# Early projections in 64-row tiles over two banks each, and an own bank for the last half block

## The chip, the cores and the metric

One Trainium2 chip, one core of it. The metric is the device time of one execution in microseconds. Matrix products run on TensorE (PE in the profile), with weight loads listed apart (PEld). VectorE is DVE, ScalarE is ACT, GpSimd is POOL, and SyncE (SP) issues the transfers. "Banks" are the eight accumulation banks (PSUM) of 128 partitions by 512 floats, which PE writes and DVE and ACT read.

## The reference

A mixer layer on x of shape 1 x 2048 x 512, in float32: layer norm, sliding-window attention with 32 heads of width 16 and a window of 256, and a gated channel MLP beside it.

```python
    x = A_x
    xn = _layernorm(x, axis=-1)
    s = _A_ref(xn, A_wqkv, A_wo)            # qkv = xn @ wqkv; softmax over the window; o @ wo
    g = _silu(_B_ref(xn, B_w1, B_b1, B_w2, B_b2))   # layer norm again, gelu(y @ w1 + b1) @ w2 + b2
    return x + s * g
```

## The kernel before

**Arithmetic.** Products with float32 accuracy are made of three passes over operands split into a high and a low part (`PASSES`). A projection job is therefore 12 matmuls of 512 columns (four slices of 128 rows times three passes) or 24 of 256.

**Slots.** The attention runs in slots t = 0 to 127, one block of 128 keys of one group of four heads each. `prob_block` makes scores (`stb`), which ACT turns into exponentials (`pt`) and POOL masks. `max_block(m)`, twelve slots ahead (`LEAD = 12`, m = t + 12), makes scores for the row maxima: four matmuls into `xy`, four into `zo`, then on DVE a masked copy (`COPY_PREDICATED`) and a `TENSOR_REDUCE`. `xy` is one tile, so the next block's matmuls wait for that reduction. Slots -16 to -1 have no exponentials; there the maxima of the first group are found while the first projections are made.

**Fill work.** The projections are cut into pieces and hung into half slots (t, 0) and (t, 1) in the table `fills`: `job_qk(n, c)` projects queries and keys of head group n for the 512 tokens of chunk c, `job_v(hf, i)` projects values for 256 tokens, and `job_x(c)` transposes the normalised x of chunk c, which the projections of that chunk need. A job's `finish` copies the result out of its bank; `later(k, ...)` puts a step k half slots on. For `job_qk(0, c)` the high part is cast by ACT and the low part subtracted by DVE straight from the bank, so the bank is free only behind both.

**Order.** Every engine but SP runs its instructions in the order in which the code was written; nothing is rescheduled. A step that waits holds back all that stands behind it on its engine.

**Banks.** `xy`, `zo` and `fb[0]`, `fb[1]` hold two, two and one each; before slot 0 the pool `ps_st` has two more, which become `stb` at slot 0.

**Rows of the array.** The score matmuls (`xy`, most of `zo`, `stb`) use tiles of 64 rows, two of which run side by side on the two halves of the array. From slot 3 on `tandem` runs two projection jobs in the same way: in a first phase the lower rows of one job and the upper rows of the other, in a second phase the reverse, into `fb[0]` and `fb[1]`. Ahead of slot 3 the projections use all 128 rows.

**The end.** `end_chunk` multiplies the attention's result by wo, 12 matmuls for a block of 128 tokens, and DVE gates it. The last block is cut in two halves of 256 columns, both in one tile `ps`, so that the first can be gated and sent while the second is made.

## Time and profile before

| what | us |
|---|---|
| median of three runs | 737.28 (737.04 to 737.39) |
| the profiled execution, its own time | 736.97 |
| its span in the trace | 735.2 |
| PE busy in the span | 722.8 |
| slots -8 to -1 (start of the first fill of -8 to the first `stb`) | 34.1 to 61.8 |
| slots 0 to 2 | 61.8 to 71.5 |

All times of the trace count from the start of the span. A line of the timeline gives start, length, engine, line, operation, output and inputs, shape and count, and in brackets the idle time before it and what ended it. All instructions pass through one helper (L43), so groups are told apart by tile names: `fb`, `pv` and `tr` are banks of projections and transposes, `pjr` and `sh` the low and high parts of a query and key projection, `xnT` the transposed x, `vt` the values, `wqb` and `wva` weights.

### The profile page before, as it was taken

The page shows a single profiled execution, that of the slowest core. Times are in us where ns is not written, and L with a number is a line of the kernel's source. Part 1 is how long each engine was busy: PE and PEld are TensorE (multiplying, and loading weights), DVE is VectorE, ACT ScalarE, POOL GpSimd, SP SyncE. Part 2 cuts the span into 40 slices and gives each one's busy share as a digit, 9 for nine tenths or more (in the row PEclk, how much of TensorE's full clock was granted, in tenths as well). Part 3 has the DMA queues.
Part 4 walks back from the last instruction along what each step waited for, and adds up shares of the span by engine and source line. Part 5 has one row for each costly group of instructions (what it writes and reads, how often), then busy time and mean ns, then how long its engine had stood idle before and what let it go on. Part 6 is the DMA issues. An engine that isn't in the chain of part 4 may idle for free.

```text
span 735.2 us, 18562 instructions
## 1 busy us (share of the span) xinstructions
PE 722.8 (98%) x7344; PEld 583.7 (79%) x7344; DVE 498.4 (68%) x736; ACT 425.3 (58%) x713; POOL 315.8 (43%) x669
## 2 busy tenths in 40 slices
PE   8999999999999999999999999999999999999997
PEld 7886777777778888777776788888888888888886
DVE  7886777877766676777872657446787855667823
ACT  7757777868777676788877736232343734541001
POOL 7413757867677665777877540203302000001102
PEclk9999999999999999999999999999999999999999
DMA  8333356877676733677624367447223312263701
GB/s 286 88 68 76 84 144 167 224 213 222 200 202 177 209 113 107 158 178 205 177 82 143 129 230 181 162 130 243 86 58 115 115 59 86 67 191 112 247 14 58
DMA packets 61526, 106.74 MB, mean 145 GB/s; under 512 B 12096, under 2 KB 12352, under 8 KB 61440
## 3 DMA queue, kind: packets, MB, share of 16 engines
q1 hardware_dynamic: 61440, 105.56, 49.1%
q8 instruction: 58, 0.95, 0.5%
q14 instruction: 28, 0.23, 0.1%
HBM read 54.53 MB, written 33.82 MB: 120 GB/s over the span
## 4 chain that ended last, share of the span: by engine, by line
PE 93%; ACT 3%; DVE 2%; issue 1%; DMA 1%; SPq 0%; DVEq 0%; ACTq 0%
PE fb L43 20%; PE acc L43 20%; PE zo L43 14%; PE stb L43 9%; PE p L43 9%; PE s L43 6%; PE h L43 6%; PE xy L43 6%; PE pv L43 3%; ACT pt L43 2%; DMA x<-in_x_dram 1%; DVE xy L43 0%; PE tr L43 0%; DVE xnT L43 0%; ACT x L43 0%
## 5 line engine op out<-in xcount | busy, mean ns | idle before, releaser
L43 POOL TENSOR_SCALAR_AFFINE_SELECT pt<-pt 128x256 f32<-128x256 f32 x480 | 192.9, 426 | 121.2 <-ACT pt L43 116.0
L43 ACT ACTIVATE pt<-stb 128x768 f32<-128x768 f32 (+1 forms) x244 | 188.7, 773 | 45.2 <-PE stb L43 38.3
L43 DVE TENSOR_REDUCE mt<-xy 128x4 f32<-128x1024 f32 (+1 forms) x128 | 152.6, 1192 | 4.4
L43 DVE COPY_PREDICATED xy<-upper,zo 128x512 f32<-128x512 int32 x112 | 77.8, 695 | 74.2 <-PE xy L43 66.8
L43 POOL TENSOR_TENSOR xo<-xo,gated 128x512 f32<-128x512 f32 x15 | 19.9, 1330 | 221.5 <-DVE gated L43 220.5
L43 PE MATMUL fb<-xnT,wqb 64*128 64x512 f32 (+1 forms) x684 | 106.6, 397 | 0.1
L43 PE MATMUL zo<-pt,vt 128*17 128x128 f32 x2880 | 103.6, 275 | 0.0
L43 PE MATMUL stb<-qk 64*128 64x384 f32 (+1 forms) x488 | 95.0, 384 | 5.1 <-ACT pt L43 4.0
L43 PE MATMUL acc<-w,gh 128*128 128x512 f32 x320 | 98.5, 389 | 0.0
L43 PEld LDWEIGHTS stb<-qk 64*128 64x128 f32 x488 | 45.7, 183 | 50.0 <-ACT pt L43 40.9
L43 PEld LDWEIGHTS zo<-pt,vt 128*17 128x17 f32 x2880 | 67.5, 97 | 15.2 <-issue 4.9
L43 PEld LDWEIGHTS fb<-xnT,wqb 64*128 64x128 f32 (+1 forms) x684 | 64.6, 185 | 8.7 <-issue 0.6
L43 PEld LDWEIGHTS acc<-w,gh 128*128 128x128 f32 x320 | 60.1, 188 | 12.5
L43 PE MATMUL acc<-w,gl 128*128 128x512 f32 x160 | 62.4, 390 | 0.2 <-DVE gl L43 0.2
L43 PE MATMUL xy<-qk 64*128 64x256 f32 (+2 forms) x536 | 58.5, 291 | 0.2 <-DVE mt L43 0.2
L43 PEld LDWEIGHTS xy<-qk 64*128 64x128 f32 x536 | 46.6, 185 | 6.8 <-issue 3.1
L43 PE MATMUL p<-xnT 128*128 128x512 f32 x189 | 51.8, 389 | 0.0
L43 ACT COPY oraw<-zo 128x128 f32<-128x128 f32 x108 | 28.7, 266 | 38.3 <-PE zo L43 29.3
L43 ACT ACTIVATE gated<-acc 128x512 f32<-128x512 f32 x16 | 8.7, 596 | 62.4 <-DVE acc L43 62.4
L43 PE MATMUL s<-wos,ohl 128*128 128x512 f32 (+1 forms) x204 | 44.3, 376 | 0.0
L43 PEld LDWEIGHTS s<-wos,ohl 128*128 128x128 f32 x204 | 36.8, 188 | 7.1
L43 PEld LDWEIGHTS p<-xnT 128*128 128x128 f32 x189 | 35.5, 188 | 7.4
(178 smaller groups left out, 1156.5 us busy)
## 6 DMA issues: line engine op xcount, KB each, us to landing
qk<-sh SPq DMA_DIRECT2D x128, 128.0 KB
qk<-pjr SPq DMA_DIRECT2D x64, 128.0 KB
oT_d<-oraw SPq DMA_DIRECT2D x32, 256.0 KB
w_d<-in_w_dram SPq DMA_DIRECT2D x14, 512.0 KB
xt_d<-xnT SPq DMA_DIRECT2D x12, 512.0 KB
x<-in_x_dram SPq DMA_DIRECT2D x16, 256.0 KB
w<-w_d SPq DMA_DIRECT2D x16, 256.0 KB
or<-oT_d SPq DMA_DIRECT2D x16, 256.0 KB
```

The lines of the kernel that those rows point to most:

```text
L43: r = issue(*args, **kwargs)
```

## The change

From slot -8 on, every projection up to slot 2 is run by the new `by_halves`. A job's 512 columns (or two blocks of 256) lie in two banks. In the first phase a unit is a matmul of the upper 64 rows into the second bank and one of the lower 64 rows into the first; in the second phase the rows change banks. A job is then 24 units of two matmuls of 64 rows by 256 columns. Between the phases stands a hand-over: POOL sets one column of `sv` to zero once the first phase's last two matmuls are through, and the second phase's first two wait for that.

```diff
+    def by_halves(job, banks, first, second):
+        half, finish, box = job
+        box[:] = banks
+        seen = []
+        for phase, where in enumerate((first, second)):
+            for i in range(12):
...
+                    two = (half(box[1 - phase], 1 - phase, i, slice(64, P), **flags),
+                           half(box[phase], phase, i, slice(0, 64), **flags))
+                    if phase == 0 and i == 11:
+                        seen.append(nc.gpsimd.memset(sv[:, 31:32], 0.0))
+                        for r in two:
+                            tc.add_manual_dep(seen[0].ins, r.ins.name, ORDER, reason="the rows are through")
+                    if phase == 1 and i == 0:
+                        for r in two:
+                            tc.add_manual_dep(r.ins, seen[0].ins.name, ORDER, reason="the banks change rows")
+                fills.setdefault(where[len(where) * i // 12], []).append((unit, ()))
+        fills[second[-1]].append((finish, ()))
```

The jobs' places are written out in pairs, whose phases alternate:

```diff
-    groups = [(4 * c - 16, 4, group(c)) for c in range(NCH)]
-    for t0, n, jobs in groups:
-        fills.update(spread(jobs, [(t0 + i // 2, i % 2) for i in range(2 * n - (t0 == -4))]))
-    fills[-8, 0] += fills[-8, 1][:4]
-    del fills[-8, 1][:4]
+    for c in range(2):
+        fills.update(spread(group(c), [(4 * c - 16 + i // 2, i % 2) for i in range(8)]))
...
+    others = [free_bank, free_bank]
+    for job, banks, first, second in (
+            (job_qk(0, 2), fb, [(-8, 0)], [(-7, 0)]), (job_v(0, 4), others, [(-8, 1)], [(-7, 1)]),
+            (job_v(0, 5), fb, [(-5, 0)], [(-4, 0)]), (job_qk(0, 3), others, [(-5, 1)], [(-4, 1)]),
+            (job_v(0, 6), fb, [(-3, 0)], [(-2, 0)]), (job_qk(1, 0), others, [(-3, 1)], [(-2, 1)]),
+            (job_v(0, 7), fb, [(-1, 0)], [(-1, 1)]), (job_qk(1, 1), fb, [(0, 1), (1, 0)], [(2, 0), (2, 1)])):
+        by_halves(job, banks, first, second)
+    fills.update(spread([job_x(3)], [(-6, 0), (-6, 1)]))
```

The transposes of the last chunk, `job_x(3)`, use `fb[0]` and `fb[1]` for their first two quarters (the second and third before) and `ps_st` for the other two. A job's `finish` copies from two banks with two instructions. For `job_qk(1, 0)` and `(1, 1)` the copies were one instruction each. Before, `job_qk(1, 0)` and `(1, 1)` were spread over slots -2 to 2: 10 of their 24 matmuls stood ahead of slot 0. Now `(1, 0)` ends in slot -2 and `(1, 1)` begins in slot 0.

The last block's second half goes to a tile of another pool:

```diff
-            ps = ps_st.tile([P, 512], F32, tag="b", name=f"s_{c}_{i}")
+            halves = []
             for cols in parts:
                 k = 0
+                ps = (ps_yt if halves else ps_st).tile([P, 512], F32, tag="b", name=f"s_{c}_{i}_{len(halves)}")
+                halves.append(ps)
...
-                    nc.vector.tensor_mul(gated[:, i, h], ps[:, h], gated[:, i, h])
+                    nc.vector.tensor_mul(gated[:, i, h], halves[q][:, h], gated[:, i, h])
```

Three places of the order of instructions, before and with the change. Words in brackets name the engines or transfers for which an instruction waits.

POOL, from the end of slot -9: the layer norm of the last chunk (`x_93` is the tile with its tokens), and what follows it. Before:

```order
L43 TENSOR_SCALAR ve_3_565<-sums 128x1 [waits Activation_49]
L43 TENSOR_TENSOR rss<-ve_3_565,mhalf 128x1 [waits Pool_49]
L43 TENSOR_SCALAR x_93<-x_93,nm_230,rss 128x512 [waits DMAHW1_49]
L43 TENSOR_SCALAR x_93<-x_93,nm_230,rss 128x512 [waits DMAHW2_49,Pool_49]
L43 AFFINE_SELECT pt_0_1_868<-pt_0_1_868 128x2x128 [waits Activation_49]
```

With the change:

```order
L43 TENSOR_SCALAR ve_3_565<-sums 128x1 [waits Activation_49]
L43 TENSOR_TENSOR rss<-ve_3_565,mhalf 128x1 [waits Pool_49]
L43 TENSOR_SCALAR x_93<-x_93,nm_230,rss 128x512 [waits DMAHW1_49]
L43 TENSOR_SCALAR x_93<-x_93,nm_230,rss 128x512 [waits DMAHW2_49,Pool_49]
L43 MEMSET sv 128x1 [waits PE_49]
L43 MEMSET sv 128x1 [waits PE_49,Pool_49] x6
L43 AFFINE_SELECT pt_0_1_1100<-pt_0_1_1100 128x2x128 [waits Activation_49]
```

The seven hand-overs ahead of slot 0 stand behind the layer norm on POOL; the eighth follows among the selections.

PE, slots -6 and -5: the transposes of the last chunk with the maxima of m = 6 between, and the first matmuls behind them. Before (`pv_4`, `pv_5` are the values' tiles, `tr` are tiles of `ps_st`, `fb_111` and `fb_112` the two `fb` banks):

```order
L43 MATMUL pv_4_607<-wva,xnT 128x256 x12
L43 MATMUL tr_0_646<-ident,x_93 128x128 [waits Activation_49,Pool_49]
L43 MATMUL tr_0_646<-ident,x_93 128x128 [waits Pool_49] x3
L43 MATMUL fb_111<-ident,x_93 128x128 x4
L43 MATMUL xy<-qk_94 128x256 [waits DVE_49]
L43 MATMUL xy<-qk_94 128x256 x3
L43 MATMUL zo<-qk_94 128x128 x4
L43 MATMUL fb_112<-ident,x_93 128x128 x4
L43 MATMUL tr_3_675<-ident,x_93 128x128 [waits Activation_49]
L43 MATMUL tr_3_675<-ident,x_93 128x128 x3
L43 MATMUL pv_5_683<-wva,xnT 128x256 [waits DVE_49]
```

With the change:

```order
L43 MATMUL fb_111<-ident,x_93 128x128 [waits DVE_49]
L43 MATMUL fb_111<-ident,x_93 128x128 x3
L43 MATMUL fb_112<-ident,x_93 128x128 [waits DVE_49]
L43 MATMUL fb_112<-ident,x_93 128x128 x3
L43 MATMUL xy<-qk_94 128x256 x4
L43 MATMUL zo<-qk_94 128x128 x4
L43 MATMUL tr_2_734<-ident,x_93 128x128 [waits Activation_49]
L43 MATMUL tr_2_734<-ident,x_93 128x128 x3
L43 MATMUL tr_3_741<-ident,x_93 128x128 [waits Activation_49]
L43 MATMUL tr_3_741<-ident,x_93 128x128 x3
L43 MATMUL fb_112<-wva,xnT 128x256 [waits DVE_49]
```

The first two quarters now go to the banks that the query and key job has just left, and the values' job behind the transposes begins in the banks of these two quarters.

DVE, from the reduction of m = 4 to that of m = 6. Before:

```order
L43 TENSOR_REDUCE mt_4_586<-xy 128x4 [waits DVE_49]
L43 TENSOR_TENSOR pjr_2_600<-fb_112,sh_2_599 128x512 [waits Activation_49]
L43 COPY_PREDICATED xy<-upper,zo 128x4x128 [waits DVE_49,PE_49]
L43 TENSOR_REDUCE mt_4_586<-xy 128x4 [waits DVE_49]
L43 TENSOR_TENSOR xnT<-tr_0_646,xnT 128x512 [waits Activation_49]
L43 COPY_PREDICATED xy<-upper,zo 128x4x128 [waits DVE_49,PE_49]
L43 TENSOR_REDUCE mt_4_586<-xy 128x4 [waits DVE_49]
L43 TENSOR_TENSOR xnT<-fb_111,xnT 128x512 [waits Activation_49]
```

With the change:

```order
L43 TENSOR_REDUCE mt_4_601<-xy 128x4 [waits DVE_49]
L43 COPY_PREDICATED xy<-upper,zo 128x4x128 [waits DVE_49,PE_49]
L43 TENSOR_REDUCE mt_4_601<-xy 128x4 [waits DVE_49]
L43 TENSOR_TENSOR pjr_2_664<-fb_111,sh_2_663 128x256 [waits Activation_49]
L43 TENSOR_TENSOR pjr_2_664<-fb_112,sh_2_663 128x256 [waits Activation_49]
L43 TENSOR_TENSOR xnT<-fb_111,xnT 128x512 [waits Activation_49]
L43 COPY_PREDICATED xy<-upper,zo 128x4x128 [waits DVE_49,PE_49]
L43 TENSOR_REDUCE mt_4_601<-xy 128x4 [waits DVE_49]
L43 TENSOR_TENSOR xnT<-fb_112,xnT 128x512 [waits Activation_49]
```

The subtraction that frees the query and key job's banks stands one reduction later, in two instructions; the one that frees the second transposed quarter's bank still stands behind the reduction of m = 6.

More of the change, by code (lines that the diff above doesn't have):

```diff
@@ L233, in mm @@
             if i == 0:
-                box.append([fb[0], fb[1], zo[:, 0], None][kt] if c == 1 and kt < 3 else fill_bank() if c > 1 and kt in (1, 2) else
+                box.append([fb[0], fb[1], zo[:, 0], None][kt] if c == 1 and kt < 3 or c == 3 and kt < 2 else
+                           fill_bank() if c == 2 and kt in (1, 2) else
                            ps_st.tile([P, 512], F32, tag="b", name=f"tr_{c}_{kt}"))
@@ L297, in mm @@
             if i == 0:
-                box.append(fill_bank() if n or c else xy[:, 0])
+                box.append(fill_bank() if c else xy[:, 0])
             kt, a, b = ops[i]
@@ L301, in mm, with half @@
                              start=(i == 0), stop=(i == len(ops) - 1))
+        def half(bank, j, i, r, **flags):
+            kt, a, b = ops[i]
+            return nc.tensor.matmul(bank[:, 0:256], wqs[n][r, a, kt],
+                                    big[r, b, kt, 512 * c + 256 * j: 512 * c + 256 * (j + 1)], **flags)
         def send(src, qk, tt):
@@ L309, in finish @@
             lo = raw.bitcast(F32R)
-            src = raw if n else box[0]
             if n:
-                nc.scalar.copy(raw, box[0])
+                for j, bank in enumerate(box):
+                    nc.scalar.copy(raw[:, 256 * j: 256 * (j + 1)], bank[:, 0:256])
+                box[:] = [raw]
+            wide = 512 // len(box)
+            parts = [(bank[:, 0:wide], slice(wide * j, wide * (j + 1))) for j, bank in enumerate(box)]
             def high():
-                nc.scalar.copy(hi, src)
+                for src, at_ in parts:
+                    nc.scalar.copy(hi[:, at_], src)
                 behind(now[0], send_high)
@@ L322, in low @@
             def low():
-                (nc.gpsimd if n else nc.vector).tensor_tensor(lo, src, hi.bitcast(F32), op=ALU.subtract)
+                for src, at_ in parts:
+                    (nc.gpsimd if n else nc.vector).tensor_tensor(lo[:, at_], src, hi[:, at_].bitcast(F32),
+                                                                  op=ALU.subtract)
                 behind(now[0], send_low)
@@ L330, in finish, with unit @@
             later(1 if n else 0, high)
-            later(3 if n else 1, low)
+            later(3 if n else int(c < 3), low)
+        if n or c > 1:
+            return half, finish, box
         return [(216, mm, i) for i in range(len(ops))], finish
+    def by_halves(job, banks, first, second):
[4 more added lines that the diff above has]
+            for i in range(12):
+                flags = dict(start=(phase == 0 and i == 0), stop=(phase == 1 and i == 11), skip_group_check=True)
+                def unit(i=i, phase=phase, flags=flags):
+                    if phase == 0 and i == 0:
+                        box[:] = [bank() if callable(bank) else bank for bank in box]
+                    two = (half(box[1 - phase], 1 - phase, i, slice(64, P), **flags),
[9 more added lines that the diff above has]
+        fills[second[-1]].append((finish, ()))
     def job_v(hf, i):
@@ L344, in mm, with half @@
                              start=(k % 12 == 0), stop=(k % 12 == 11))
+        def half(bank, j, k, r, **flags):
+            kt, (a, b) = k // 3, PASSES[k % 3]
+            kb = 2 * i + j
+            return nc.tensor.matmul(bank[:, 0:256], big[r, a, kt, P * kb: P * (kb + 1)], wva[r, b, kt], **flags)
         def finish():
-            nc.scalar.copy(vt[:, 2 * i: 2 * i + 2, :, 0:DH], box[0].rearrange("p b (h d) -> p b h d", d=DH))
+            if i < 4:
+                nc.scalar.copy(vt[:, 2 * i: 2 * i + 2, :, 0:DH], box[0].rearrange("p b (h d) -> p b h d", d=DH))
+                return
+            for j, bank in enumerate(box):
+                nc.scalar.copy(vt[:, 2 * i + j, :, 0:DH], bank[:, 0:256].rearrange("p (h d) -> p h d", d=DH))
+        if i > 3:
+            return half, finish, box
         return [(109, mm, k) for k in range(24)], finish
@@ L741, in group, with free_bank @@
             return [job_qk(0, 0), job_v(0, 0), (ops[:12] + x_ops, lambda: None), (ops[12:], finish)]
-        return [job_qk(0, c), job_v(0, 2 * c), *([job_x(c + 1)] if c + 1 < NCH else []), job_v(0, 2 * c + 1)]
-    groups = [(4 * c - 16, 4, group(c)) for c in range(NCH)]
-    for t0, n, jobs in groups:
-        fills.update(spread(jobs, [(t0 + i // 2, i % 2) for i in range(2 * n - (t0 == -4))]))
-    fills[-8, 0] += fills[-8, 1][:4]
-    del fills[-8, 1][:4]
+        return [job_qk(0, c), job_v(0, 2 * c), job_x(c + 1), job_v(0, 2 * c + 1)]
+    for c in range(2):
+        fills.update(spread(group(c), [(4 * c - 16 + i // 2, i % 2) for i in range(8)]))
+    def free_bank():
+        return ps_st.tile([P, 512], F32, tag="b", name=f"pair_{now[0]}")
+    others = [free_bank, free_bank]
[6 more added lines that the diff above has]
+    fills.update(spread([job_x(3)], [(-6, 0), (-6, 1)]))
     fills[-10, 0][:0] = fills[-11, 1][-5:]
     del fills[-11, 1][-5:]
-    for place, todo in spread([job_qk(1, 0), job_qk(1, 1)], [(-2, 0), (-1, 1), (-1, 1), (-1, 1), (0, 0), (0, 1)] +
-                              [(t, k) for t in (1, 2) for k in range(2)]).items():
-        fills.setdefault(place, []).extend(todo)
-    fills[0, 1].insert(0, fills[0, 0].pop())
     soon = {}
```

## The prediction

> **What bounds the kernel now.** First the page: the busy shares and the chain that ended last.

> ```profile
> span 735.2 us, 18562 instructions
> PE 722.8 (98%) x7344; PEld 583.7 (79%) x7344; DVE 498.4 (68%) x736; ACT 425.3 (58%) x713; POOL 315.8 (43%) x669
> PE 93%; ACT 3%; DVE 2%; issue 1%; DMA 1%; SPq 0%; DVEq 0%; ACTq 0%
> ```

> PE is the bound nearly everywhere, so what PE loses in a slot is found again at the end. But the change sits in two stages, and there I read the busy times by windows: the columns are PE, PEld, DVE, ACT and POOL.

> ```profile
> 34.10:61.80 27.70, 27.70 (x212) 23.79 (x210) 22.24 (x31) 16.42 (x24) 5.58 (x12) 1.00 0.27 60
> 61.80:71.50 9.70, 9.68 (x79) 5.70 (x78) 6.59 (x10) 6.66 (x11) 4.99 (x11) 1.00 0.36 86
> ```

> In slots -8 to -1 PE is busy without a gap for 27.70 us, but DVE is close behind with 22.24. Whatever makes PE faster there can bring 5.5 us at most, and any order in which PE and DVE wait for each other by turns brings less. The timeline of PE shows the places (start, length, what):

> ```profile
> 33.86 0.33 PE L43 MATMUL zo<-qk 64*128 64x128 f32 x4
> 34.12 2.56 PE L43 MATMUL fb<-xnT,wqb 128*128 128x512 f32 x10
> 36.61 0.50 PE L43 MATMUL xy<-qk 64*128 64x256 f32 x4
> 36.95 0.34 PE L43 MATMUL zo<-qk 64*128 64x128 f32 x4
> 37.22 0.72 PE L43 MATMUL fb<-xnT,wqb 128*128 128x512 f32 x2
> ...
> 41.48 0.60 PE L43 MATMUL tr<-ident,x 128*128 128x128 f32 x4
> ...
> 42.44 0.51 PE L43 MATMUL xy<-qk 64*128 64x256 f32 x4
> 42.78 0.34 PE L43 MATMUL zo<-qk 64*128 64x128 f32 x4
> 43.05 0.66 PE L43 MATMUL fb<-ident,x 128*128 128x128 f32 x4
> 43.55 0.60 PE L43 MATMUL tr<-ident,x 128*128 128x128 f32 x4
> 43.90 1.67 PE L43 MATMUL pv<-wva,xnT 128*128 128x256 f32 x12
> ...
> 61.81 0.44 PE L43 MATMUL stb<-qk 64*128 64x384 f32 x2
> ...
> 71.53 0.44 PE L43 MATMUL stb<-qk 64*128 64x384 f32 x2
> ```

> **What the change saves on PE.** The new unit, two matmuls of 64 x 256 side by side, already runs later in the kernel, next to score matmuls of 64 rows:

> ```profile
> 71.81 0.40 PE L43 MATMUL xy<-qk 64*128 64x256 f32 x4
> 72.04 1.08 PE L43 MATMUL fb<-xnT,wqb 64*128 64x512 f32 x8
> ...
> 97.43 0.37 PE L43 MATMUL zo<-qk 64*128 64x128 f32 x4
> 97.60 1.17 PE L43 MATMUL fb<-xnT,wqb 64*128 64x512 f32 x8
> ...
> 233.96 1.12 PE L43 MATMUL fb<-wva,xnT 64*128 64x256 f32 x16
> 234.92 0.34 PE L43 MATMUL stb<-qk 64*128 64x384 f32 x2
> ```

> Eight units from 233.96 to 234.92: 0.12 us each, so a half job of 12 is 1.44 and a job 2.88. A values' job of 24 matmuls of 128 rows has about the same pace (12 in 1.67 with the last one's tail). Ten matmuls of a query and key job took 2.49 (34.12 to 36.61), so a job about 3.0. The gain is in the changes: ahead of 64-row work `xy` costs 0.23 from start to start (71.81 to 72.04), behind 128-row work 0.34 (36.61 to 36.95); `zo` costs 0.17 (97.43 to 97.60) against 0.27 (36.95 to 37.22). A block of maxima `xy` + `zo` is thus 0.40 instead of 0.61. Eight such blocks in slots -8 to -1, all but the one between the transposes: 7 x 0.21 = 1.5 us, and the two fills of each of slots 0 to 2 change rows too, about as often (6 x 0.2 = 1.2). About 2.7 us is what there is to gain on PE.

> **What it makes PE wait for.** I put the new order on the old clock, from 33.86 on. The first half of `job_qk(0, 2)` runs from 34.03 to 35.47. The next `xy` needs the reduction of m = 3:

> ```profile
> 34.97 1.23 DVE L43 TENSOR_REDUCE mt<-xy 128x4 f32<-128x1024 f32 x1
> ```

> It ends at 36.20, so `xy` starts at 36.25, 0.8 lost; before it started at 36.61 anyway. With `zo` to 36.65; the first half of `job_v(0, 4)` to 38.09. Now the second half of the query and key job waits for the hand-over on POOL, and POOL is not free:

> ```profile
> 38.42 0.19 POOL L43 TENSOR_SCALAR ve<-sums 128x1 f32<-128x1 f32 x1
> 38.70 0.55 POOL L43 TENSOR_TENSOR rss<-ve,mhalf 128x1 f32<-128x1 f32 x1
> 39.24 1.53 POOL L43 TENSOR_SCALAR x<-x,nm,rss 128x512 f32<-128x512 f32 x2
> 63.23 0.77 POOL L43 TENSOR_SCALAR_AFFINE_SELECT pt<-pt 128x256 f32<-128x256 f32 x2 [22.46 <-ACT pt L43]
> ```

> The hand-over is written in slot -8, behind the layer norm of slot -9, whose last step ends at 40.77; that work hangs on ACT's squares and not on PE, so it comes no earlier. The hand-over itself, one column, has no row in this trace. From below it is nothing, from above the 0.55 of the small power; it is nearest to the 0.19 of a one-column multiply, and with a wait at both ends I take 0.25. PE goes on at 41.02, having lost 2.93. Behind that wait stand all of PE's later matmuls, the next `xy` among them, so DVE waits too. From 63.23 back POOL is idle for 22.46, so the next six hand-overs find it free, each at least a block of maxima ahead of its use.

> [...]

> Then, with the second half (to 42.46), `xy`, `zo` (42.86) and the second half of `job_v(0, 4)`, PE is at 44.30 with the transposes, whose banks are those of the query and key job. DVE must first do the maxima of m = 5 and then the low parts:

> ```profile
> 43.39 0.69 DVE L43 COPY_PREDICATED xy<-upper,zo 128x512 f32<-128x512 int32 x1
> 44.11 1.23 DVE L43 TENSOR_REDUCE mt<-xy 128x4 f32<-128x1024 f32 x1
> 45.25 1.28 DVE L43 TENSOR_TENSOR xnT<-fb,xnT 128x512 fp32r<-128x512 f32 x2
> ...
> 730.75 0.42 DVE L43 TENSOR_TENSOR gated<-s,gated 128x256 f32<-128x256 f32 x1 [2.18 <-PE s L43]
> ```

> From the masked copy to the subtraction behind the reduction it is 1.86 (43.39 to 45.25). `zo` of m = 5 ends at about 43.0, so the first subtraction starts at 44.9 and at 0.42 for 256 columns ends at 45.3: PE loses 1.0. Eight transposes 0.96 (41.48 to 42.44), maxima with changed rows 0.61 (42.44 to 43.05), eight more 0.85 (43.05 to 43.90): PE is at 47.8. `job_v(0, 5)` starts in both `fb` banks and needs the second quarter's subtraction, which stands behind the reduction of m = 6. That masked copy comes at 47.2 (behind the first quarter's four transposes to 46.0, its cast by ACT and its subtraction, about 0.6 each), the reduction is over at 49.06, the subtraction (half of 1.28) at 49.7: PE loses 2.0 and starts at 49.8. Before, the same job started at 43.90, on a bank of `ps_st`; PE is 5.9 late.

> From here ten half jobs (14.4) and five blocks of maxima (2.0) lead to slot 0: 66.2 instead of 61.81, **4.4 late**, with the work of two more 512-column matmuls (0.5) done.

> In slots 0 to 2 one job of 24 units (2.9) stands in place of 14 matmuls of 512 columns, and ACT becomes the limit:

> ```profile
> 59.95 1.92 ACT L43 ACTIVATE qk<-vt 128x2048 fp32r<-128x2048 f32 x1
> 62.34 0.81 ACT L43 ACTIVATE pt<-stb 128x768 f32<-128x768 f32 x1 [0.47 <-ACT qk L43]
> ```

> `stb` is one tile: 0.44 of scores, 0.81 of exponential and two waits make 1.35 a step, six steps 8.1. Before the first, ACT has still to copy the values' last job out of two banks, behind the clearing of 1.92; I add an estimate of 0.6 for it, a subtraction's length: 8.7 against 71.53 - 61.81 = 9.72. The delay shrinks by 1.0 to **3.4 at slot 3**. From there the order is the old one and PE is the bound, so it stays.

> **The end.**

> ```profile
> 719.45 11.19 PE L43 MATMUL s<-wos,ohl 128*128 128x512 f32 x60
> ...
> 731.21 0.42 DVE L43 TENSOR_TENSOR xo<-xo,gated 128x256 f32<-128x256 f32 x1
> 731.55 0.42 DVE L43 TENSOR_TENSOR gated<-s,gated 128x256 f32<-128x256 f32 x1
> ```

> PE is done at 730.64 and the first half's product starts at 730.75, though its twelve matmuls were done 1.4 us earlier: sharing the tile made it wait for both halves. With two tiles only the second half's two steps are left then: 731.55 - 730.75 = 0.80 less, and the last transfer goes that much earlier. No row speaks against this term.

> **Sum.** 3.4 - 0.8 = +2.6 on the profiled execution's 736.97, and as much on the median, which is 0.3 above it: 737.28 + 2.6 = **739.9**. The hand-over's bounds (0 to 0.55), and up to 1 us either way for the slots 0 to 2 (six exponentials alone 8.1, or the old 9.72), give the forecast 738.9 to 741.2.

> **The rivals.**
> *The hold on POOL does not bind* (the hand-over is done ahead of the layer norm, or that norm runs earlier). Then 2.93 falls away and the two waits for DVE stay: 739.9 - 2.9 = 737.0, no change. For it: POOL has 5.58 busy in 27.7. Against: the order of rows on POOL, and the 40.77.
> *PE waits for nothing new* (the banks come free in time as well): another 3.0 less, 734.0, the 2.7 of changed rows and the 0.8 of the end minus small change. For it: DVE has 5.5 us of room. Against: both subtractions stand behind reductions that wait for PE's own late `xy` and `zo`. It decides if PE's gap at the transposes is under 0.2.
> *The clock falls*: PE idles 2.9, 1.0 and 2.0 within 12 us, as it does nowhere in this trace after the start.

> ```profile
> 1.30 5.07 PE L43 MATMUL zo<-upper 128*128 128x128 f32 x22 [1.30 <-DVE zo L43]
> 7.20 0.61 PE L43 MATMUL zo<-ident 128*128 128x128 f32 x4
> ```

> Coming from idle, 22 small matmuls took 5.07, 0.23 each, while four later took 0.61, about 0.11 from start to start: 2.6 lost at that start. Once more here would give 742.5. Against: no gap is as long as the whole wait at the start, and the columns above grant 1.00. [...]
> *The halves do not run side by side*, since both take the same weights: 168 units ahead of slot 0 would each cost another 0.12, 20 us. The 0.12 of the row at 233.96 speaks against it.

> **How the numbers follow.** Forecast 0.74, POOL not binding 0.11, no new wait 0.08, clock 0.06, not side by side 0.01. What can be told from no change here is 0.2%, 1.5 us: same is 735.8 to 738.8. Faster is the third case, with a little of the second: 0.09. Same is the rest of the second and the lowest edge of the forecast: 0.13. Slower: 0.78. The range from 737.0 to 741.8 takes in the second case at its foot and leaves out the third and most of the fourth.

> **What would show it.** In the changed profile: on PE, a gap that POOL's clearing of `sv` ends, at about 41, of 2.5 to 3.2; one ended by DVE's `pjr` of about 1.0 ahead of the transposes and one by `xnT` of about 2 ahead of the values' job; the first `stb` at 66 to 67 and the first of slot 3 at 74.5 to 75.5; at the end the first half's product ahead of PE's last matmul. Wrong would be the forecast if the first `stb` came before 64, or if the delay at slot 3 did not last to the end.

## The result, and the profile after

The changed kernel takes 741.11 us (median of 4 executions, 740.91 to 741.86). The kernel before, timed beside it, takes 737.16 (736.84 to 737.39). The ratio is 1.0056, 95% interval 1.0038 to 1.0073: slower by 3.95 us, where the forecast was 2.6.

The page of the changed kernel: the span, the busy shares and the chain that ended last.

```profile
span 739.5 us, 19069 instructions
PE 721.0 (98%) x7584; PEld 587.6 (79%) x7584; DVE 500.4 (68%) x738; ACT 425.7 (58%) x721; POOL 316.9 (43%) x677
PE 88%; ACT 5%; DVE 2%; DMA 1%; issue 1%; POOL 1%; SPq 0%; ACTq 0%; DVEq 0%; POOLq 0%
```

PE is busy for 1.8 us less than before (721.0 against 722.8) and the span is 4.3 longer. So most of the new time is waiting (PE's busy time also holds what a slower clock costs, see below), and the chain shows with whom: POOL, absent before, has a share, and ACT's went from 3% to 5%.

The timeline of PE in the stage of the change (start, length, what, and in brackets the idle time before it and its releaser). A pair of banks of the pool `ps_st` is called `pair` there, and is left out here.

```profile
34.19 0.33 PE L43 MATMUL zo<-qk 64*128 64x128 f32 x4
...
36.58 0.51 PE L43 MATMUL xy<-qk 64*128 64x256 f32 x4 [0.57 <-DVE mt L43]
...
41.20 1.75 PE L43 MATMUL fb<-xnT,wqb 64*128 64x256 f32 x24 [2.46 <-POOL sv L43]
42.74 0.64 PE L43 MATMUL xy<-qk 64*128 64x256 f32 x4
43.17 0.53 PE L43 MATMUL zo<-qk 64*128 64x128 f32 x4
...
46.24 0.98 PE L43 MATMUL fb<-ident,x 128*128 128x128 f32 x7
...
50.75 1.69 PE L43 MATMUL fb<-wva,xnT 64*128 64x256 f32 x24 [1.79 <-DVE xnT L43]
...
68.01 0.34 PE L43 MATMUL stb<-qk 64*128 64x384 f32 x2
...
76.89 0.44 PE L43 MATMUL stb<-qk 64*128 64x384 f32 x2
```

The stage begins 0.33 later in this execution than in the one of before (34.19 against 33.86 for the same `zo`), which is earlier than anything that the change touches. From that row on I count: the first `stb` comes 33.82 later (before 27.95), the first of slot 3 42.70 later (before 37.67). So PE is 5.9 late at slot 0 and 5.0 late at slot 3. Two waits stand out, one for POOL's hand-over and one for DVE, as forecast. The third, for DVE ahead of the transposes (46.24), isn't there. In its place something else is: between the first two waits PE runs slowly. `xy` and `zo` took 0.75 from 42.74 to the next unit at 43.49, instead of 0.40.

The same stretch in windows (length, then busy time of PE, PEld, DVE, ACT, POOL, the granted clock of PE, the DMA share and GB/s):

```profile
39.28:42.69 3.41, 1.49 (x24) 1.49 (x26) 0.00 (x0) 0.00 (x0) 1.96 (x5) 1.00 0.02 5
42.69:46.10 3.41, 3.41 (x36) 3.38 (x32) 2.33 (x4) 0.65 (x2) 0.00 (x0) 0.50 0.35 74
46.10:49.51 3.41, 2.86 (x28) 2.25 (x24) 2.19 (x4) 2.62 (x6) 0.00 (x0) 1.00 0.72 160
49.51:52.92 3.41, 2.17 (x36) 2.17 (x38) 2.40 (x5) 0.64 (x2) 0.10 (x1) 1.00 0.00 1
```

For 3.41 us the clock was granted at half. That is 1.7 of lost work. It came with a gap of 2.46, 1.92 of which lies in the 3.41 ahead of the fall.

On POOL the hand-over stands where the order of instructions put it, behind the layer norm:

```profile
39.58 1.52 POOL L43 TENSOR_SCALAR x<-x,nm,rss 128x512 f32<-128x512 f32 x2
41.05 0.25 POOL L43 MEMSET sv<- 128x1 f32 x2
52.56 0.10 POOL L43 MEMSET sv<- 128x1 f32 x1 [11.26 <-PE fb L43]
```

At the end the first half's product now starts ahead of PE's last matmul, which ends at 735.74 (724.55 + 11.19):

```profile
734.41 0.42 DVE L43 TENSOR_TENSOR gated<-s,gated 128x256 f32<-128x256 f32 x1 [0.74 <-PE s L43]
734.87 0.45 DVE L43 TENSOR_TENSOR xo<-xo,gated 128x256 f32<-128x256 f32 x1
735.78 0.42 DVE L43 TENSOR_TENSOR gated<-s,gated 128x256 f32<-128x256 f32 x1 [0.45 <-PE s L43]
736.24 0.42 DVE L43 TENSOR_TENSOR xo<-xo,gated 128x256 f32<-128x256 f32 x1
```

DVE is done 0.92 behind PE (736.66 - 735.74); before it was 1.79 (its last step at 732.00 + 0.43, PE's end at 730.64). The end thus saves 0.87.

### The profile page after: what moved, and what is told of

The parts are those of the page before. It is cut to its first block, busy times and chain, and to the rows that moved or that the text cites. A ratio compares the mean times of both kernels' runs of the same rounds, so it can differ in the third digit from the quotient of the medians.

```text
span 739.5 us, 19069 instructions
## 1 busy us (share of the span) xinstructions
PE 721.0 (98%) x7584; PEld 587.6 (79%) x7584; DVE 500.4 (68%) x738; ACT 425.7 (58%) x721; POOL 316.9 (43%) x677
## 3 DMA queue, kind: packets, MB, share of 16 engines
HBM read 54.53 MB, written 33.82 MB: 119 GB/s over the span
## 4 chain that ended last, share of the span: by engine, by line
PE 88%; ACT 5%; DVE 2%; DMA 1%; issue 1%; POOL 1%; SPq 0%; ACTq 0%; DVEq 0%; POOLq 0%
PE acc L43 20%; PE fb L43 19%; PE zo L43 13%; PE stb L43 9%; PE p L43 9%; PE s L43 6%; PE h L43 6%; PE xy L43 5%; ACT pt L43 3%; PE pv L43 1%; DMA wvr<-in_wv_dram 1%; DVE xnT L43 1%; ACT qk L43 1%; DMA qk<-pjr 1%; DVE xy L43 0%
## 5 line engine op out<-in xcount | busy, mean ns | idle before, releaser
L43 POOL TENSOR_SCALAR_AFFINE_SELECT pt<-pt 128x256 f32<-128x256 f32 x480 | 192.8, 426 | 100.7 <-ACT pt L43 95.3
L43 ACT ACTIVATE pt<-stb 128x768 f32<-128x768 f32 (+1 forms) x244 | 188.7, 773 | 45.7 <-PE stb L43 39.5
L43 DVE TENSOR_REDUCE mt<-xy 128x4 f32<-128x1024 f32 (+1 forms) x128 | 152.6, 1192 | 4.4
L43 DVE COPY_PREDICATED xy<-upper,zo 128x512 f32<-128x512 int32 x112 | 77.9, 695 | 77.9 <-PE xy L43 65.2
L43 POOL TENSOR_TENSOR xo<-xo,gated 128x512 f32<-128x512 f32 x15 | 19.9, 1330 | 220.5 <-DVE gated L43 219.5
L43 PE MATMUL zo<-pt,vt 128*17 128x128 f32 x2880 | 103.7, 275 | 0.0
L43 PE MATMUL fb<-xnT,wqb 64*128 64x512 f32 (+2 forms) x732 | 99.3, 381 | 2.5 <-POOL sv L43 2.5
L43 PE MATMUL stb<-qk 64*128 64x384 f32 (+1 forms) x488 | 95.2, 384 | 5.6 <-ACT pt L43 4.3
L43 PE MATMUL acc<-w,gh 128*128 128x512 f32 x320 | 98.6, 389 | 0.0
L43 PEld LDWEIGHTS stb<-qk 64*128 64x128 f32 x488 | 45.8, 184 | 49.2 <-ACT pt L43 40.5
L43 PEld LDWEIGHTS zo<-pt,vt 128*17 128x17 f32 x2880 | 67.5, 97 | 15.2 <-issue 4.9
L43 PEld LDWEIGHTS acc<-w,gh 128*128 128x128 f32 x320 | 60.1, 188 | 12.4
L43 PEld LDWEIGHTS fb<-xnT,wqb 64*128 64x128 f32 (+1 forms) x732 | 62.8, 186 | 8.8 <-POOL sv L43 2.7
L43 PE MATMUL acc<-w,gl 128*128 128x512 f32 x160 | 62.4, 390 | 0.2 <-DVE gl L43 0.2
L43 PE MATMUL xy<-qk 64*128 64x256 f32 (+2 forms) x536 | 58.4, 291 | 1.2 <-DVE mt L43 1.1
L43 PEld LDWEIGHTS xy<-qk 64*128 64x128 f32 x536 | 46.7, 186 | 6.6 <-issue 2.5
L43 PE MATMUL p<-xnT 128*128 128x512 f32 x189 | 51.8, 389 | 0.0
L43 ACT COPY oraw<-zo 128x128 f32<-128x128 f32 x108 | 28.7, 266 | 36.9 <-PE zo L43 26.8
L43 ACT ACTIVATE gated<-acc 128x512 f32<-128x512 f32 x16 | 8.7, 596 | 62.4 <-DVE acc L43 62.4
L43 PE MATMUL s<-wos,ohl 128*128 128x512 f32 (+1 forms) x204 | 44.3, 377 | 0.0
L43 PEld LDWEIGHTS s<-wos,ohl 128*128 128x128 f32 x204 | 36.8, 188 | 7.1
L43 PEld LDWEIGHTS p<-xnT 128*128 128x128 f32 x189 | 35.5, 188 | 7.4
```

The costliest lines, as they stand in the source:

```text
L43: r = issue(*args, **kwargs)
```

## The experiments

Two questions were open: what of the 3.95 belongs to the waits and what to the clock, and whether the halves are worth anything once the waits are gone. Twelve runs were made, in four groups, each group beside the kernel before on one chip. The table gives all of them; the stage columns count from the `zo` used above, in the profiled execution, and a fall is a stretch of 3.41 at clock 0.50 ahead of PE's last matmul.

| kernel | median (lowest to highest) | before beside it | ratio, 95% interval | to first `stb` | to slot 3 | falls in its trace |
|---|---|---|---|---|---|---|
| before | | | | 27.95 | 37.67 | 0 |
| the change | 741.11 (740.91 to 741.86) | 737.16 | 1.0056 (1.0038 to 1.0073) | 33.82 | 42.70 | 1 |
| the change again | 742.14 (742.01 to 742.95) | 737.33 | 1.0067 (1.0055 to 1.0080) | 35.63 | 44.48 | 2 |
| end alone | 736.62 (736.31 to 737.30) | 737.37 | 0.9990 (0.9982 to 0.9999) | 27.95 | 37.66 | 0 |
| halves alone | 743.28 (742.93 to 744.04) | 737.37 | 1.0081 (1.0067 to 1.0095) | 34.79 | 43.63 | 1 |
| hand-over on ACT | 740.06 (738.19 to 740.40) | 737.37 | 1.0032 (1.0021 to 1.0044) | 32.47 | 41.32 | 1 |
| one filler | 742.21 (740.58 to 742.46) | 737.37 | 1.0056 (1.0042 to 1.0070) | 34.87 | 43.73 | 1 |
| DVE's steps earlier | 740.06 (738.91 to 740.43) | 737.33 | 1.0034 (1.0021 to 1.0046) | 32.91 | 41.77 | 1 |
| both | 736.51 (736.18 to 737.71) | 737.33 | 0.9990 (0.9982 to 0.9999) | 29.15 | 38.01 | 0 |
| slots 0 to 2 and the end | 735.10 (734.88 to 736.05) | 737.33 | 0.9972 (0.9963 to 0.9982) | 28.42 | 36.74 | 0 |
| hold of 2.5 in before | 741.12 (739.42 to 742.79) | 737.29 | 1.0053 (1.0040 to 1.0066) | 30.41 | 40.11 | 0 |
| hold of 1.1 in before | 737.97 (737.68 to 738.23) | 737.29 | 1.0010 (1.0001 to 1.0019) | 28.87 | 38.60 | 0 |
| two fillers | 741.05 (740.97 to 742.24) | 737.29 | 1.0057 (1.0044 to 1.0070) | 34.21 | 43.07 | 0 |
| two fillers, cut | 740.54 (740.02 to 740.64) | 737.14 | 1.0042 (1.0029 to 1.0056) | 33.29 | 42.14 | 0 |

**The end alone.** The kernel before with the last half block's own bank and nothing else:

```diff
-            ps = ps_st.tile([P, 512], F32, tag="b", name=f"s_{c}_{i}")
...
+                ps = (ps_yt if halves else ps_st).tile([P, 512], F32, tag="b", name=f"s_{c}_{i}_{len(halves)}")
...
```

> The kernel before with the last block's second half in its own tile, and nothing else. Theory (two parts that add up): the first half's product no longer waits for PE's last matmul, the last two DVE steps are all that is left behind it, -0.8 us: about 736.4 against 737.2. Rival (the last transfer sets the end, not DVE): no change, 737.2.

737.37 - 736.62 = 0.75, as forecast; the interval of the ratio (0.9982 to 0.9999) excludes the rival's "no change". The end is settled.

**The halves alone.** The change with the shared tile of before at the end.

```diff
+            ps = ps_st.tile([P, 512], F32, tag="b", name=f"s_{c}_{i}")
...
-                ps = (ps_yt if halves else ps_st).tile([P, 512], F32, tag="b", name=f"s_{c}_{i}_{len(halves)}")
...
```

> The changed kernel with both halves of the last block in one tile again. Theory: the early slots alone cost 3.95 + 0.8 = 4.7 us: about 741.9, and the first scores of slot 3 stand where they stand in the changed kernel (76.9). Rival (the end brought nothing): 741.1, as the changed kernel.

It lost 5.9, more than either theory. In its trace both waits for DVE are there and the clock falls in another place, behind the second of them. Three windows of 3.41, laid on the fall:

```profile
40.31:43.72 3.41, 2.10 (x34) 2.10 (x36) 0.00 (x0) 0.36 (x2) 1.36 (x4) 1.00 0.03 5
...
47.13:50.54 3.41, 1.72 (x17) 1.39 (x16) 3.07 (x5) 2.35 (x5) 0.00 (x0) 1.00 0.55 123
50.54:53.95 3.41, 3.31 (x32) 3.31 (x32) 1.24 (x3) 0.00 (x0) 0.10 (x1) 0.50 0.00 0
```

So the clock had a part that neither theory priced, and its fall isn't tied to the hold on POOL.

**The first hand-over on ACT**, which is idle then:

```diff
-                        seen.append(nc.gpsimd.memset(sv[:, 31:32], 0.0))
+                        seen.append(nc.scalar.copy(sv[:, 31:32], mhalf[:, 0:1]) if now[0] == -8 else nc.gpsimd.memset(sv[:, 31:32], 0.0))
```

> The changed kernel with the first hand-over alone, that of slot -8, made by ACT (a copy of one column) in place of POOL's clearing; the other seven stay on POOL. Theory (POOL's layer norm holds the hand-over, and the clock falls in the gap): PE's gap shrinks from 2.5 us to under 1, the granted clock of 41 to 46 stays at 1.0, and the waits for DVE ahead of the transposes (about 1) and of the values' job (about 2) remain: 737.9 to 738.6, some 2.5 to 3.2 less than the changed kernel's 741.1. Rival (the banks that wait for DVE set the pace, and PE would only wait there longer): over 740.

The gap of 2.46 is gone, the waits of 0.99 and 1.79 for DVE stay. Five of six executions took 739.7 to 740.4, and one 738.19, with a mean granted clock of 1.000 where the five have 0.997 or 0.998. The one is inside the theory's 737.9 to 738.6. The median, 740.06, is the rival's "over 740", but with a clock that fell, which the rival doesn't have. In the profiled one, of the five, the clock fell behind the wait of 1.79:

```profile
44.63:48.04 3.41, 1.62 (x18) 1.31 (x18) 3.18 (x5) 2.24 (x5) 0.00 (x0) 1.00 0.49 111
48.04:51.45 3.41, 3.41 (x32) 3.41 (x34) 1.13 (x2) 0.00 (x0) 0.10 (x1) 0.50 0.00 0
```

**One filler.** Eleven products into `zo` that nothing reads keep PE busy in the hold:

```diff
+    def keep_busy():
+        for _ in range(11):
+            nc.tensor.matmul(zo[:, 0, 384:512], ident, ident, start=True, stop=True)
+    fills[-7, 0].insert(0, (keep_busy, ()))
```

> The changed kernel with eleven extra matmuls of 128 x 128 into an unused corner of zo, ahead of the second half of the first query and key job, so that PE is busy while it waits for POOL. Theory (the gap lowers the granted clock, and the slow matmuls behind it cost): the clock of 41 to 46 stays at 1.0 in place of 0.66 and twelve units take 1.4 us in place of 2.7; part of the 1.7 us comes back as a wait for DVE of about 1 ahead of the transposes: 0.5 to 1.0 less than the changed kernel, 740.1 to 740.6. Rival A (the clock costs nothing, since DVE sets the pace there): 741.1 or a little more. Rival B (the clock fell for another reason, the 64-row units themselves): it falls here too, and the time stays.

The clock stays at 1.00 where it had fallen, the wait of 0.91 ahead of the transposes is back, and the clock falls at 50.65 instead of 42.69, behind the wait of 1.79. Three executions took 742.2 to 742.5; two, with the clock at 0.999 or more, took 740.6 and 740.9. The median, 742.21, is above all that was expected: where the clock fell, keeping PE busy in one gap only moved the fall.

**DVE's steps earlier.** Two steps that had been put one half slot on are not delayed:

```diff
-                later(int((c, kt) in ((2, 2), (2, 3), (3, 1))),
+                later(int((c, kt) in ((2, 2), (2, 3))),
...
-            later(3 if n else int(c < 3), low)
+            later(3 if n else int(c < 2), low)
```

> The changed kernel with two steps of DVE put one half slot earlier, ahead of the reductions that held them: the low part of the query and key job of chunk 2 and the subtraction of the second transposed quarter. The hand-over stays on POOL. Theory (a hold on POOL, two waits for DVE, and a clock that falls behind such waits): the 1.79 at the values' job goes to under 0.5, the POOL gap of about 2.5 stays. If the clock still falls behind that gap, 741.1 - 1.8 = 739.3; in an execution in which it does not fall, 739.3 - 1.6 = 737.7, clock 0.999 or more. Rival 'the hold on POOL is all of it, the waits for DVE cost nothing that lasts': as the changed kernel, 741.1.

The wait of 1.79 went and the one at POOL (2.48) stayed. 740.06 is 2.1 below the change run beside it (742.14), so DVE's waits do cost. Two of five executions, at a clock of 0.999 or more, took 738.9 and 739.3. The theory's own figures, 739.3 and 737.7, were both too low, having been taken from 741.1.

**Both of these** edits together, all else as in the change:

> As the kernel before it with the two DVE steps earlier, and the first hand-over made by ACT in place of POOL; the halves, their places and banks stay as in the change. Theory: no wait of PE over 0.8 between slots -8 and 0 is left, the clock stays at 1.00 in each stage and the gain in changes of rows shows: the run with the hand-over on ACT and no fall of the clock took 738.2; less 1.0 and 1.8 for the two waits is 735.4, bounds 735.2 to 736.6. Rival 'units of 64 rows cost the clock by themselves, whatever waits stand there': the clock column falls under 0.95 somewhere from 34 to 68 and the time is 737.0 to 738.2. Rival 'the halves bring nothing, the changes of rows cost no time here': 737.4 - 0.75 = 736.6 or more at an unfallen clock.

What PE still waits for from 34 to 72:

```profile
PE xy L43 <- DVE mt L43: 1.1, 3, 0.6
PE stb L43 <- ACT pt L43: 0.5, 2, 0.3
PE pair_-5_786 L43 <- DVE xnT L43: 0.2, 1, 0.2
```

All eleven executions are at 0.999 or more: here the units of 64 rows didn't bring the clock down. But 736.51 is the time of the kernel with the end alone (736.62), at the upper end of the theory's 735.2 to 736.6 and on the rival's 736.6. Slot 0 is reached 1.2 later than before, 0.5 of which is work that stood behind it before (two matmuls of 512 columns); by slot 3 it is still 0.3. So even without long waits the halves ahead of slot 0, in these places, win nothing.

**Slots 0 to 2 and the end.** The kernel before, with only `job_qk(1, 1)` by halves, `job_qk(1, 0)` (128 rows) done ahead of slot 0, and the end's bank:

```diff
-    for place, todo in spread([job_qk(1, 0), job_qk(1, 1)], [(-2, 0), (-1, 1), (-1, 1), (-1, 1), (0, 0), (0, 1)] +
-                              [(t, k) for t in (1, 2) for k in range(2)]).items():
+    for place, todo in spread([job_qk(1, 0)], [(-2, 0), (-1, 1), (-1, 1), (-1, 1)]).items():
...
-    fills[0, 1].insert(0, fills[0, 0].pop())
+    by_halves(job_qk(1, 1), fb, [(0, 0), (0, 1)], [(1, 0), (1, 1), (2, 0), (2, 1)])
```

> The kernel before with two parts of the change alone: the second group's second query and key job by halves in slots 0 to 2 (its first job ends ahead of slot 0, with 128 rows as before), and the last half block's own bank. All of slots -8 to -3 as in the kernel before. Theory: no hold on POOL and no wait for DVE that was not there before, clock 1.00 throughout; slots 0 to 2 give back 0.8 to 1.7 as in the change, two more matmuls of 512 columns stand ahead of slot 0 (0.5), the end 0.75: 737.4 - 0.75 - 0.3 to 737.4 - 0.75 - 1.7, that is 734.9 to 736.3. Rival 'the halves in slots 0 to 2 bring nothing, ACT sets those slots': 736.6.

This is faster than both kernels: 735.10, ratio 0.9972 (0.9963 to 0.9982). Slots 0 to 2 take 8.32 instead of 9.72, for 0.47 more ahead of them. The first and last rows of that stage, and its only wait of over 0.25:

```profile
62.35 0.44 PE L43 MATMUL stb<-qk 64*128 64x384 f32 x2
...
69.20 0.44 PE L43 MATMUL stb<-qk 64*128 64x384 f32 x2 [0.31 <-ACT pt L43]
70.67 0.44 PE L43 MATMUL stb<-qk 64*128 64x384 f32 x2
```

**The change again**, beside the three above.

> The changed kernel again, on the same chip as the three above. Theory: 741.1, with a mean granted clock of 0.997 or 0.998 in executions in which it falls, and about 1.6 less (739.5) in any in which it stays at 0.999 or more. Rival 'the clock has no part in the time': executions with and without the fall take the same.

No execution was without a fall, so the rival is not refuted by this run alone. The profiled one took 742.95 and shows two falls, one behind each long wait:

```profile
38.81:42.22 3.41, 1.00 (x16) 1.00 (x18) 0.45 (x1) 0.00 (x0) 2.38 (x6) 1.00 0.02 5
42.22:45.63 3.41, 3.41 (x36) 3.41 (x36) 1.43 (x2) 0.65 (x2) 0.00 (x0) 0.50 0.09 21
...
49.05:52.46 3.41, 1.62 (x26) 1.44 (x26) 3.08 (x5) 1.37 (x3) 0.00 (x0) 1.00 0.07 16
52.46:55.87 3.41, 3.41 (x38) 3.41 (x36) 2.14 (x4) 0.00 (x0) 0.10 (x1) 0.50 0.01 2
```

The two begin 10.24 apart (42.22 and 52.46), three times 3.41.

**A hold in the kernel before.** No halves, only a hand-over on POOL in the middle of the values' job (0, 4), ahead of its seventh matmul in one kernel and of its thirteenth in the other:

```diff
...
+            if (hf, i, k) == (0, 4, 5):
+                held.append(nc.gpsimd.memset(sv[:, 31:32], 0.0))
+                tc.add_manual_dep(held[0].ins, r.ins.name, ORDER, reason="the hold")
+            if (hf, i, k) == (0, 4, 6):
+                tc.add_manual_dep(r.ins, held[0].ins.name, ORDER, reason="the hold")
```

> The kernel before, computing all that it did, with one thing added: the seventh matmul of the values' job (0, 4) waits for a clearing of one column of sv on POOL, as the change's first hand-over does. No halves, no moved job, no change at the end. PE would be at that matmul at about 38.5 and goes on at about 41.05: a gap of 2.5. Theory (a granted clock that falls to half for 3.4 us where about half of the 3.4 us ahead was idle on PE, cost up to 1.7): 737.3 + 2.5 + 1.7 = 741.5 with a mean clock of 0.997 or 0.998 in most executions, 739.8 at 0.999 or more in the few where the gap is cut by the check. Rival 'units of 64 rows, not the idling, bring the clock down': no execution below 0.999, 739.8. Rival 'the hold is made good later by DVE's room': under 738.5.

> As the kernel before it in this call, but the hold is put on the thirteenth matmul of the values' job, which PE reaches at about 39.95: a gap of 1.1. Theory: too short for the clock, every execution at 0.999 or more, 737.3 + 1.1 = 738.4. Rival 'any stop of PE brings the clock down, or brings it down by chance': some executions at 0.998 or less, 740.1.

The long one made a gap of 2.21 and took 739.42 and 739.76 (clock 0.999), 741.02 and 741.23 (0.997), 742.52 and 742.79 (0.995): three levels, about 1.5 apart. The lowest is the hold itself, +2.3, which DVE's room doesn't make good. The others are one fall and two, by the mean clock. The profiled execution is of the lowest level, so where the falls of the others lie isn't seen.

```profile
40.94 0.98 PE L43 MATMUL pv<-wva,xnT 128*128 128x256 f32 x6 [2.21 <-POOL sv L43]
```

Why its gap of 2.21 passed without a fall can be estimated. In the profile of the change a fall begins at 42.69 and, PE done, another at 739.01, 204 steps of 3.4133 (a third of the 10.24 above) apart. In the trace of the long hold the clock falls at 735.91, PE done (mean clock 0.999); 204 such steps back lies 39.59, inside the gap. A window's edge there splits it, and each of the two windows has more than half its length of work:

```profile
36.18:39.59 3.41, 2.54 (x19) 1.82 (x17) 2.80 (x7) 2.10 (x5) 2.41 (x8) 1.00 0.03 5
39.59:43.00 3.41, 2.06 (x18) 1.86 (x19) 0.80 (x2) 0.00 (x0) 1.29 (x3) 1.00 0.74 158
```

The short one made a gap of 0.84 and took +0.68, within 0.6 from the lowest to the highest: no fall that costs time. One execution, the profiled one, has a mean clock of 0.998, which the expectation excluded; its windows read 1.00 until 733.5, and the fall there comes when PE has finished. So in these runs idling alone was enough for a lower clock (0.995 to 0.997 in four of the long hold's six executions), without any of the change's units of 64 rows, and a gap of 0.84 wasn't.

**Two fillers**, in both long waits:

```diff
     fills[-7, 0].insert(0, (keep_busy, ()))
+    fills[-5, 0].insert(0, (keep_busy, ()))
```

> The changed kernel with 11 products of 128x128 into zo, which nothing reads, ahead of the second half of the query and key job (as in the run with one filler) and 11 more ahead of the values' job (0, 5): PE is kept busy in both long waits, which stay as they are. Theory: no stretch of 3.4 us is idle for half any more, every execution at 0.999 or more, and the change without any fall of the clock takes what the two unfallen runs with one filler took, 740.6 to 740.9. Rival 'the clock falls for another reason than idling': executions at 0.997 or 0.998 and 742.2 remain.

All five executions are at 0.999 or more: with PE busy in both waits no fall is left, whatever the waits cost. (One took 742.24, 1.2 above the median at a clock of 1.000; why isn't known, and any single execution named here may be off by as much.) But the second filler, from 48.01 to 50.66, is longer than the wait that it covers, so I cut both (10 and 7 products):

> The kernel with two fillers, with these cut to the waits: 10 products ahead of the second half of the query and key job in place of 11, and 7 ahead of the values' job in place of 11, whose 2.65 were 0.9 longer than the wait of 1.8 that they cover. Theory: every execution at 0.999 or more, the values' job starts when DVE lets it, and the change without any fall of the clock takes 741.05 - 0.9 = 740.1, which is near the forecast's 739.9. Rival 'the change costs 741 without the clock as well, and the forecast missed 1.2 elsewhere': 741.0 at 0.999 or more.

```profile
45.65 1.09 PE L43 MATMUL fb<-ident,x 128*128 128x128 f32 x8 [0.91 <-DVE pjr L43]
...
48.31 1.83 PE L43 MATMUL zo<-ident 128*128 128x128 f32 x14
50.17 1.70 PE L43 MATMUL fb<-wva,xnT 64*128 64x256 f32 x24
```

740.54 (740.02 to 740.64), half way between the theory's 740.1 and the rival's 741.0: the change without a fall costs 740.54 - 737.14 = 3.4, and each of the two answers has half of what was missing.

## Why the prediction was right, and where its size was off

**The hold on POOL.** Right. Forecast 38.09 to 41.02, a loss of 2.93; measured 38.74 to 41.20, 2.46. POOL's rows stand in the order of the program, the clearing (41.05) behind the layer norm (39.58). Counted from the same `zo`, PE came to the wait 0.32 later than forecast and left it 0.15 earlier; the hand-over's price was set too high, 0.25 against 0.10 for a single one. With the hand-over on ACT and no fall, one execution took 738.19, 2.3 less than the change without falls. The rival "POOL does not bind" is refuted, and so is its arithmetic: without the hold the time is not 737.0.

**The waits for DVE.** Right, 0.91 and 1.79 against 1.0 and 2.0, where the clock doesn't fall in between. In the profiled execution of the change the first is missing because PE was slow: it reached the transposes when DVE was done. In the kernel with cut fillers the values' job starts 16.0 after the first `zo` (50.17 - 34.16, the `zo` of that execution); the forecast was 15.9 (49.8 - 33.86). Up to here nothing was missed.

**4.4 late at slot 0: too small.** Without a fall it is 33.29 - 27.95 = 5.3. The signs named for it, the first `stb` at 66 to 67 and slot 3 at 74.5 to 75.5, did not come (68.01 and 76.89). The term that was too small is "ten half jobs (14.4) and five blocks of maxima (2.0)": the change took 68.01 - 50.75 = 17.26 for these 16.4. Of the 0.9 some 0.4 is one stop, which the row of the weight loads names (with the step on DVE that it waits for):

```profile
59.97 0.18 PEld L43 LDWEIGHTS pair_-3_931<-xnT,wqb 64*128 64x128 f32 x1 [0.31 <-DVE wqb L43]
...
59.23 0.68 DVE L43 TENSOR_TENSOR wqb<-wqkr,wqb 128x512 fp32r<-128x512 f32 x1
```

The change moves `job_qk(1, 0)` from slot -2 to slot -3, while the low part of that group's weights stays where it was, and the sum hadn't asked when these weights are ready. The other half is small: the first unit behind a block of maxima takes 0.17 instead of 0.12, a block 0.42 instead of 0.40, the half job that follows the wait of 1.79 takes 1.52 (50.75 to 52.27) and the last one 1.53 (66.48 to 68.01) instead of 1.44.

**Slots 0 to 2.** Forecast 1.0 back, measured 9.72 - 8.88 = 0.84; the two waits for `pt` that ACT ends are there, and ahead of them one of 0.32 for a reduction, which the sum didn't have. **The end.** Forecast 0.80, measured 0.75 by itself.

**The sum without a fall** is then 5.3 - 0.9 - 0.8 = 3.6 in the profiled execution, 3.4 by the medians, against 2.6.

**The clock** is the rest, and the step of the prediction that failed is its "Against" in that rival. It took the wait at the kernel's start as the nearest row, found no gap as long (1.30 of that wait lie in the span, and no row shows more of it), and left the fall at 0.06 as an alternative to the forecast; it came in addition to it, in all nine executions of the change, by their times and mean clocks (0.995 to 0.998) and by the two traces. A gap of 2.46 was enough. In all the traces with a fall, laid on windows of 3.41, PE was busy for 1.00 to 1.72 in the window ahead of it; of the windows cut the same way with 2.10 or more (2.17 in the change, from 49.51) none was followed by one. The window of the long hold with 2.06 wasn't either, nor one of 1.79 as PE finishes in the kernel with cut fillers (733.40 to 736.81, PE's last matmul done at 735.19, clock 1.00 behind it, mean clock 1.000). So a fall followed where PE had idled for 1.69 or more of the 3.41 ahead (1.72 busy), and none where it had idled for 1.62 or less (1.79 busy). The edges lie elsewhere in each execution (one at 42.69 and one at 42.22 in the two traces of the change). That a gap of 1.8 to 2.5 is cut in two by an edge in some executions and not in others is an estimate from these figures; in the executions without a trace no edge was seen.

A fall cost 1.7, half of 3.41, where PE was the bound, and less where a wait followed that it swallowed. Counted to slot 3, against 42.14 without a fall: one behind the hold 42.70, so 0.6, since the wait of 0.91 went with it; one behind the hold and one behind the wait of 1.79, 44.48, so 2.3 = 0.6 + 1.7. That fits the same kernel's 740.9 to 741.9 in one set of runs and 742.0 to 743.0 in another (one fall behind the hold 740.5 + 0.6, one behind the wait of 1.79 740.5 + 1.7, both 740.5 + 2.3), but one execution of each set was profiled, so for the others the place of the fall is not shown. The prediction's 2.6 for one fall was too much.

**Luck.** The direction and the waits were foreseen. That 741.11 lies inside the forecast's 738.9 to 741.2 is in part luck: 0.8 was missing from the sum, and the fall that it didn't have happened to stand where it cost 0.6. The second set's 742.14 is outside, and above the 741.8 of the range too.

**"PE waits for nothing new", 734.0.** Both long waits can be taken away, and the time is 736.5. The forecast's 1.5 us of gain from changes of rows in slots -8 to -1 does not show there, though the blocks of maxima did get shorter (0.42 against 0.61). The waits that its trace names there (0.57 and 0.19 for the reductions, 0.2 for `xnT`) make up 1.0. Its rows of weight loads name two more, 0.29 for the hand-over on ACT and 0.25 for `wqb`, the stop seen above; what holds the rest was not separated, and stays open.

## What to carry to other kernels

Before a hand-over is put on an engine, look at what its queue holds at that moment: a clearing of 0.10 cost 2.46 because a layer norm stood ahead of it. Where two engines feed each other by turns and the second is at 80% of the first, a faster first engine may only wait, as it did here; halves won 0.9 up to slot 3 where they were used in slots 0 to 2 alone (36.74 against 37.67), and nothing ahead of slot 0 as they were placed. Price a new gap of PE not by its length alone but with the clock behind it, which fell here from 1.69 of idling in 3.41 on, and ask for each job that is moved earlier when all of its operands, weights included, are ready.
